# Attention with soft cap and two feed-forward layers: the first pairs' AV product and row sums in column strips, casts on other engines, PSUM banks in one turn

## The chip, the cores and the metric

One core of a Trainium2 chip runs the whole program. The metric is the device time of one execution in microseconds. The times named "before" are those of the unchanged kernel: median 1199.77 us of three runs, from 1199.32 to 1201.66.

## The reference

```python
# q, k, v: (4, 12, 448, 64) float32, cap: a scalar
scores = (q @ k.T) / sqrt(64)
scores = cap * tanh(scores / cap)
attn = exp(scores - max(scores)); attn = attn / (sum(attn) + 1e-9)
x = (attn @ v)                   # heads side by side: (1792, 768)
h = x @ moe_w_in                 # (768, 2048)
x = (h * cos(h)) @ moe_w_out     # (2048, 768)
h = maximum(x @ moe2_w_in, 0)
out = (h * h) @ moe2_w_out       # (1792, 768)
```

## The kernel before

**Precision.** Most products are made of three passes with float32r operands: each operand is split into a high part (a cast) and a low part (operand minus high part), and `mm3` adds high x high, high x low and low x high in PSUM. The exception is the product of the probabilities with v in the first twelve pairs: there both operands are plain float32, and one matmul leaves two records in the trace.

**Pairs.** Two heads make a pair; four batches with six pairs each are 24 pairs, numbered n. Each pair has 448 keys in four groups g: groups 0 to 2 hold 128 keys for each of the two heads, group 3 holds the last 64 keys of both heads, one head in partitions 0 to 63 and the other in 64 to 127. Scores are kept with keys on partitions and the 448 queries along the free axis. The first twelve pairs (n < NA, two batches) are worked off by `a_first` at the start; the other twelve are cut into steps (`a_steps`) that are issued between the matmuls of the feed-forward layers of the first window (`side_step`).

**One call of a_first(n)** issues, in this order: scores of groups 0 and 1; the transposes and casts of pair n+1 (`a_prep`, L298); the loads of pair n+2; exp of groups 0 and 1; the AV product of group 2 of pair n-1; scores of groups 3 and 2; the split of x of pair n-2 (`a_x`, L431); AV of group 3 of pair n-1; the normalisation of pair n-1 (`a_out`, L411); exp of groups 3 and 2; AV of groups 0 and 1 of pair n; the load of v of pair n+1. Between them four slots take pieces of the first three weights' preparation (`W_SLOTS`). Each engine works its instructions off in this order. The scores of groups 0 to 2 are two matmuls beside each other, each in 64 of the 128 rows of the array; those of group 3 use all rows.

**AV before (a_av, L402).** `vf` holds for each head and group 64 columns of v and 64 columns of ones. Each head is a matmul of its own over 128 columns into its own bank: partitions 0 to 63 receive attn @ v, partitions 64 to 127 the sum of exp. `a_out` transposes the sums on VectorE (L417), takes the reciprocal (L422), spreads it with a second transpose (L423) and multiplies (L429), the first and the last once per head. The two banks of a pair, `acc(n)`, alternate between bM and bA; the transposes of pair n+1 use the banks of pair n before its AV begins.

**Casts.** In `a_prep` ScalarE casts k (L327), VectorE casts q and makes both low parts. In `a_x` VectorE makes both parts of x for the first twelve pairs.

**Layers and windows.** A window is two batches. It runs `layer(True)` (cosine gate, eight blocks of 128 features for both batches, sixteen PSUM groups), `layer_out` (back to 768 columns; six column blocks d, two batches b, two steps e), again the same two for the other half of the features, and then the second network's `layer(False)` (ReLU, squared) and `layer_out`, twice. `layer` takes the banks of its ring by the number of the group, `layer_out` by 2d + b; each starts at the ring's first bank. For `layer(True)` the ring has four banks, for `layer(False)` and most calls of `layer_out` three (bM and bS[3]), for the last `layer_out` of a window six. `relu_a` reads a bank on ScalarE (L571). At the end of `layer_out(o_x)`, VectorE makes the high part of x (L631) and GpSimd the low part (L632), which the following `layer(False)` reads.

**Edges.** `a_load`, `a_loadv` and the outputs issue their DMAs on SP's queue. The outputs are transposed (L645), copied by ScalarE and VectorE (L647, L648) and written by two DMAs (L650, L653).

Of the kernel before, what the change touches and what calls it, by code (L numbers as in the profile page):

```python
# [11 lines left out]
F32 = mybir.dt.float32  # L12
# [4 lines left out]
ALU = mybir.AluOpType  # L17
# [11 lines left out]
def tile_softcap_attention_moe_cos_moe_relu2(  # L29
# [59 lines left out]
    bS = [psum.tile([P, 512], F32, name=f"bS{i}") for i in range(4)]  # L89
    bM = [psum.tile([P, 512], F32, name=f"bM{i}") for i in range(2)]  # L90
    bA = [psum.tile([P, 512], F32, name=f"bA{i}") for i in range(2)]

    def hilo(hi, lo, src, eng=None):
        if eng is None:
            nc.scalar.copy(out=hi, in_=src)
        else:
            eng.tensor_copy(out=hi, in_=src)  # L97
        nc.vector.tensor_tensor(out=lo, in0=src, in1=hi.bitcast(F32), op=ALU.subtract)

# [127 lines left out]
    def rows_a(t, b, h, n=1):  # L229
        return t[b, h:h + n, 0:TA, :].rearrange("h (r c) d -> r c h d", c=4)  # L230
# [16 lines left out]
        return t if g < 3 else t[:, 0:1]  # L247


    vf = [at_p.tile([P, 7, P], F32, name=f"vf{i}", tag=("q2", "k2")[i]) for i in range(2)]  # L250

    def v_of(n):
        return vf[n % 2]
# [24 lines left out]
    def a_loadv(n):  # L278
        b, p = divmod(n % (B * NP), NP)
        h = 2 * p  # L280
        if n < NA:
            t = v_of(n)
            for j in range(2):
                nc.sync.dma_start(out=t[0:RA, 3 * j:3 * j + 3, 0:D], in_=rows_a(v, b, h + j)[:, 0:3, 0])
                nc.sync.dma_start(out=t[RA:P, 3 * j:3 * j + 3, 0:D], in_=rows_b(v, b, h + j)[:, :, 0])
                nc.sync.dma_start(out=t[RA * j:RA * j + RA, 6, 0:D], in_=rows_a(v, b, h + j)[:, 3, 0])
            return
        vr = at_p.tile([P, 7, D], F32, name="vr", tag="vr")
        v6 = vr[:, 0:6].rearrange("p (h c) d -> p h (c d)", h=2)
        va = v[b, h:h + 2, 0:TA, :].rearrange("h (r c) d -> r h (c d)", c=4)  # L290
        vb = v[b, h:h + 2, TA:S, :].rearrange("h (r c) d -> r h (c d)", c=3)
        nc.sync.dma_start(out=v6[0:RA], in_=va[:, :, 0:3 * D])
        nc.sync.dma_start(out=v6[RA:P], in_=vb)
        for j in range(2):
            nc.sync.dma_start(out=vr[RA * j:RA * j + RA, 6], in_=rows_a(v, b, h + j)[:, 3, 0])
        vraws[n] = vr

    def a_prep(n):  # L298
        qr, kraw = raws.pop(n), kraw_of(n)
        bq, bk = acc(max(n, 2) - 1) if n < NA else bS[1:3]  # L300
        for t, bank in ((kraw, bk), (qr, bq)):
            for c in range(4):
                nc.tensor.transpose(bank[:, P * c:P * c + P], t[:, c].rearrange("p h d -> p (h d)"), ident)  # L303
        if n >= NA:
            q2 = at_p.tile([P, 2, S], F32R, name="q2", tag="q2")
            k2 = at_p.tile([P, 2, 512], F32R, name="k2", tag="k2")
            hs = [slice(RA * j, RA * j + RA) for j in range(2)]
            for j in range(2):
                nc.scalar.copy(out=k2[hs[j], j], in_=bk[hs[j]])
            for j in range(2):  # L310
                nc.scalar.copy(out=q2[hs[j], j], in_=bq[hs[j], :S])
            for j in range(2):
                nc.gpsimd.tensor_copy(out=k2[hs[1 - j], j], in_=k2[hs[j], j].bitcast(F32))
            for j in range(2):
                nc.vector.tensor_tensor(
                    out=kz[hs[j], j], in0=bk[hs[j]], in1=k2[hs[j], j].bitcast(F32), op=ALU.subtract
                )
            for j in range(2):
                nc.vector.tensor_tensor(
                    out=q2[hs[1 - j], j], in0=bq[hs[j], :S], in1=q2[hs[j], j].bitcast(F32), op=ALU.subtract  # L320
                )
            qkts[n] = (q2, k2)
            return
        t = 2 + 3 * (n % 2)
        qh, ql = gt[t][:, 0], gt[t][:, 1]
        kh, kl = flat[t + 1][:, :512], flat[t + 2][:, :512]
        nc.scalar.copy(out=kh, in_=bk)  # L327
        nc.vector.tensor_copy(out=qh, in_=bq[:, :S])
        nc.vector.tensor_tensor(out=kl, in0=bk, in1=kh.bitcast(F32), op=ALU.subtract)
        nc.vector.tensor_tensor(out=ql, in0=bq[:, :S], in1=qh.bitcast(F32), op=ALU.subtract)  # L330
        qkts[n] = (qh, ql, kh, kl)
# [64 lines left out]
        pts[n, g] = ((vh, ph), (vl, ph), (vh, pl))  # L396

    def a_av(n, g):
        todo = pts.pop((n, g)) if n >= NA else ((v_of(n), t_of(n, g)),)
        for i, (a, x) in enumerate(todo):  # L400
            for j in range(2):
                first, last = g == 0 and i == 0, g == 3 and i == len(todo) - 1  # L402
                if g < 3:
                    nc.tensor.matmul(acc(n)[j][:, :S], a[:, 3 * j + g, :], x[:, j], start=first, stop=last)  # L404
                else:
                    r = slice(RA * j, RA * j + RA)
                    nc.tensor.matmul(acc(n)[j][:, :S], a[r, 6, :], x[r, 0], start=False, stop=last)  # L407

    xts = {}

    def a_out(n):  # L411
        st = at_p.tile([P, S], F32, name="st", tag="st")
        xts[n] = xx = at_p.tile([P, S], F32, name="xx", tag="xx")
        rc = at_p.tile([P, S // 32], F32, name="rc", tag="rc")
        for j in range(2):
            o = slice(RA * j, RA * j + RA)
            nc.vector.transpose(out=st[o], in_=acc(n)[j][RA:P, :S])  # L417
        sums = st.rearrange("p (a b) -> p a b", b=32)[:, :, 0]
        if tops.pop(n, None) is not None:
            nc.vector.tensor_scalar(out=rc, in0=sums, scalar1=1e-9, scalar2=None, op0=ALU.add)  # L420
            sums = rc
        nc.vector.reciprocal(out=rc, in_=sums)  # L422
        nc.vector.transpose(  # L423
            out=st.rearrange("p (a b) -> p a b", b=32),
            in_=rc.rearrange("p (a o) -> p a o", o=1).to_broadcast([P, S // 32, 32]),
        )
        for j in range(2):
            o = slice(RA * j, RA * j + RA)
            nc.vector.tensor_tensor(out=xx[o], in0=acc(n)[j][0:RA, :S], in1=st[o], op=ALU.mult)  # L429

    def a_x(n):  # L431
        b, c = divmod(n, NP)
        if WB <= b < B:
            nc.sync.dma_start(out=xkeep[n - NA], in_=xts.pop(n))
        else:
            hilo(xh[b % WB][c], xl[b % WB][c], xts.pop(n), nc.vector if n < NA else None)

    def x_back(n):
        b = n // NP
# [7 lines left out]
        nc.gpsimd.tensor_tensor(out=xl[b % WB][c], in0=t, in1=xh[b % WB][c].bitcast(F32), op=ALU.subtract)  # L447

    def a_first(n):

        slots = iter(W_SLOTS if n else ((),) * 4)
# [11 lines left out]
            a_exp(n, g)  # L465
        w_slot(next(slots))
        if n > 0:
            a_av(n - 1, 2)
        a_score(n, 3)
        a_score(n, 2)  # L470
        if n > 1:
            a_x(n - 2)
        if n > 0:
            a_av(n - 1, 3)
            a_out(n - 1)
        a_exp(n, 3)
        w_slot(next(slots))
# [1 line left out]
        w_slot(next(slots))  # L479
        for g in range(2):  # L480
            a_av(n, g)
        if 0 < n and n + 1 < B * NP:
            a_loadv(n + 1)

    def a_last(n):
        a_x(n - 1)
        for g in range(2, 4):
            a_av(n, g)
        a_out(n)
        a_x(n)  # L490

# [83 lines left out]
    def split_g(b, i, u):  # L575
        nc.scalar.copy(out=gh[b][i], in_=u)  # L576
        nc.vector.tensor_tensor(out=gl[b][i], in0=u, in1=gh[b][i].bitcast(F32), op=ALU.subtract)  # L577

    def layer(first, weave=None):
        ring = bM + bA if first else bM + bS[3:]  # L580
        w0 = wpos[0]
        order = [(i, b) for i in range(FB) for b in range(WB)]
        if weave is not None:
# [2 lines left out]
        for k, (i, b) in enumerate(order):  # L586
# [3 lines left out]
            elif k == 0:  # L590
                w_next(0)
            wh, wl = wsp[w0 + i]
            ps = ring[k % len(ring)][:, :S]
            for c in range(NCC):
                mm3(ps, wh[:, c], wl[:, c], xh[b][c], xl[b][c], c == 0, c == NCC - 1)
            if weave is not None and k == 2:
# [2 lines left out]
            (cos_a if first else relu_a)(b, i, ps)  # L599
            if k == 0 and weave is not None:  # L600
                weave()

    def layer_out(done, w=None):

        ring = bM + (bS[3:] if w is None else bS)
        w = NWIN if w is None else w
        for d in range(NCC):
            if w + 1 < NWIN:
                for b in range(WB):
                    x_back((w * WB + WB + b) * NP + d)  # L610
            for e in range(FB // OP):
                w_next(WB * OP * 3)
                wh, wl = wsp[wpos[0] - 1]
                for b in range(WB):
                    ps = ring[(WB * d + b) % len(ring)][:, :S]
                    for c in range(OP):
                        f = e * OP + c
                        mm3(ps, wh[:, c], wl[:, c], gh[b][f], gl[b][f], f == 0, f == FB - 1)
# [7 lines left out]
    def o_x(b, d, ps):  # L626
# [2 lines left out]
        nc.scalar.copy(out=u, in_=ps)  # L629
        nc.vector.tensor_tensor(out=t, in0=u, in1=t, op=ALU.add)  # L630
        nc.vector.tensor_copy(out=xh[b][d], in_=t)  # L631
        nc.gpsimd.tensor_tensor(out=xl[b][d], in0=t, in1=xh[b][d].bitcast(F32), op=ALU.subtract)  # L632

    def o_y(w):
        def done(b, d, ps):
# [5 lines left out]
    def y_tr(b, d, y):  # L641
        bk = bA[b % WB]
        for c in range(4):
# [3 lines left out]
        nc.scalar.copy(out=o[0:RA].rearrange("p c f -> p (c f)"), in_=bk[0:RA, :])  # L647
        nc.vector.tensor_copy(out=o[RA:P, 0:3].rearrange("p c f -> p (c f)"), in_=bk[RA:P, 0:3 * P])  # L648
        t0 = (b % B) * S
        nc.sync.dma_start(  # L650
            out=out[t0:t0 + TA, d * P:(d + 1) * P].rearrange("(r c) f -> r c f", c=4), in_=o[0:RA]
        )
        nc.sync.dma_start(  # L653
# [50 lines left out]
    with tc.manual_schedule():  # L704
# [3 lines left out]
            nc.vector.memset(t[0:RA, 3, 1], 0.0)  # L708
        for t in (qraw, wide_view(pg[0])):
            nc.vector.memset(t[RA:P, 3], 0.0)  # L710
        a_load(0)
        busy(11)
        nc.sync.dma_start(out=capt, in_=cap.partition_broadcast(P))
        make_identity(nc, ident)
        a_load(1)
        a_loadv(0)
        for t in vf:
            nc.gpsimd.memset(t[:, :, D:P], 1.0)
        nc.gpsimd.memset(vh[:, :, D:P].bitcast(F32), 1.0)
        nc.gpsimd.memset(vl[:, :, D:P].bitcast(F32), 0.0)  # L720
        nc.vector.scalar_tensor_tensor(
# [50 lines left out]
```

## Time and profile before

| what | value |
|---|---|
| median of three runs | 1199.77 us |
| the profiled execution's own time | 1200.93 us |
| its span | 1199.1 us |
| PE busy | 1180.7 us (98%) |
| PE weight loads busy | 1035.6 us (86%) |
| VectorE busy | 664.0 us (55%) |
| ScalarE busy | 654.1 us (55%) |
| GpSimd busy | 83.4 us (7%) |

The span runs from the first to the last instruction that the profile shows; the rest of an execution's time lies around it. PE is the matmul side of TensorE, PEld its weight loads, DVE is VectorE, ACT ScalarE, POOL GpSimd and SP the engine whose queue issues most DMAs; a "q" behind an engine's name means its sequencer or queue. Matmuls are pipelined: the recorded length of one is more than the distance to the next, so prices of passes are read from the distance between starts. A releaser is the instruction that ended a wait.

### The profile page before, as it was taken

Reading aid. Unit: us, or ns where it says so; the run is one execution under the profiler, and the core shown is the slowest. Engines: PE = TensorE matmul, PEld = TensorE weight load, DVE = VectorE, ACT = ScalarE, POOL = GpSimd, SP = SyncE. Lnnn points to the kernel's source line nnn. Section 1 sums busy time; section 2 is a strip of 40 time slices with the busy share of each in tenths; the row PEclk is TensorE's granted clock in tenths of the full one; section 3 lists DMA queues with packets and bytes.
Section 4 is the critical chain, followed back from the end, with each engine's and each line's share of the span. In section 5 each row is a group of like instructions: output and inputs, shape, how many; then the busy total and the mean of one; then the engine's idle time right before and its main releaser. Section 6 shows DMA issues by size and latency. Waiting matters only on the chain.

```text
span 1199.1 us, 15735 instructions
## 1 busy us (share of the span) xinstructions
PE 1180.7 (98%) x5835; PEld 1035.6 (86%) x5835; DVE 664.0 (55%) x1075; ACT 654.1 (55%) x1092; POOL 83.4 (7%) x86
## 2 busy tenths in 40 slices
PE   9999999999999999999999999999999999999996
PEld 5555899999988888999888999999999998999896
DVE  3886796689999888678777754400442111001121
ACT  6987674377866999677885435512541243124301
POOL 1000000000322110001001210000002100000000
PEclk9999999999999999999999999999999999999998
DMA  5544356754556545556645874234223422342152
GB/s 128 139 101 114 129 201 210 253 212 176 183 161 212 189 145 166 161 167 197 208 148 179 267 238 150 88 105 144 101 72 110 154 88 79 117 139 88 53 150 69
DMA packets 163333, 179.65 MB, mean 150 GB/s; under 512 B 64400, under 2 KB 130464, under 8 KB 163248
## 3 DMA queue, kind: packets, MB, share of 16 engines
q1 hardware_dynamic: 162256, 178.26, 46.9%
q8 instruction: 48, 0.79, 0.3%
q10 hardware_dynamic: 928, 0.23, 0.1%
q14 instruction: 37, 0.30, 0.1%
q0 software_dynamic: 64, 0.07, 0.0%
HBM read 119.93 MB, written 58.59 MB: 149 GB/s over the span
## 4 chain that ended last, share of the span: by engine, by line
PE 94%; DVE 4%; ACT 1%; issue 0%; DVEq 0%
PE bM L524 45%; PE bS L524 23%; PE bA L524 9%; PE bA L404 5%; PE bS L355 3%; PE bS L347 2%; PE bM L404 2%; PE bA L407 1%; PE bS L303 1%; PE bA L645 1%; DVE st L417 1%; DVE xx L429 1%; ACT part L360 0%; PE bM L303 0%; PE bS L700 0%
## 5 line engine op out<-in xcount | busy, mean ns | idle before, releaser
L524 PE MATMUL bM<-g,ws 128*128 128x448 f32 x1344 | 289.7, 368 | 4.8 <-ACT u L571 4.8
L524 PEld LDWEIGHTS bM<-g,ws 128*128 128x128 f32 x1344 | 252.1, 188 | 28.3 <-ACT u L571 6.3
L524 PE MATMUL bM<-xh,ws 128*128 128x448 f32 x912 | 268.3, 366 | 0.2 <-DVE xh L631 0.2
L524 PE MATMUL bS<-g,ws 128*128 128x448 f32 x960 | 210.7, 368 | 0.0
L524 PEld LDWEIGHTS bS<-g,ws 128*128 128x128 f32 x960 | 178.7, 188 | 15.2
L524 PEld LDWEIGHTS bM<-xh,ws 128*128 128x128 f32 x912 | 170.9, 188 | 16.2 <-DVE xh L97 0.7
L577 DVE TENSOR_TENSOR g<-u,g 128x448 fp32r<-128x448 f32 x128 | 80.5, 629 | 165.4 <-ACT g L576 165.4
L524 PE MATMUL bM<-xl,ws 128*128 128x448 f32 x456 | 167.4, 367 | 1.4 <-POOL xl L632 1.4
L524 PE MATMUL bA<-xh,ws 128*128 128x448 f32 x372 | 108.7, 366 | 0.0
L561 DVE SCALAR_TENSOR_TENSOR u<-kk,u 128x448 f32<-128x448 f32 x64 | 39.9, 624 | 123.5 <-ACT kk L560 123.0
L169 ACT CAST ws<-wf 128x512 fp32r<-128x512 f32 (+1 forms) x80 | 56.3, 704 | 72.6 <-DVE wf L162 28.3
L170 DVE TENSOR_TENSOR ws<-wf,ws 128x512 fp32r<-128x512 f32 (+1 forms) x80 | 64.1, 801 | 57.3 <-ACT ws L169 55.9
L524 PEld LDWEIGHTS bM<-xl,ws 128*128 128x128 f32 x456 | 85.4, 187 | 9.5 <-POOL xl L632 1.7
L576 ACT CAST g<-u 128x448 fp32r<-128x448 f32 x128 | 71.6, 560 | 8.7 <-DVE u L566 6.9
L524 PE MATMUL bS<-xh,ws 128*128 128x448 f32 x252 | 76.1, 367 | 0.0
L524 PEld LDWEIGHTS bA<-xh,ws 128*128 128x128 f32 x372 | 69.8, 188 | 6.0
L360 ACT ACTIVATE pg<-bS,small 128x448 f32<-128x448 f32 x102 | 59.4, 635 | 20.5 <-PE bS L355 15.7
L524 PE MATMUL bA<-xl,ws 128*128 128x448 f32 x186 | 68.1, 366 | 0.0
L162 DVE CUSTOM_DVE_ANT_0 wf<-wr,wf 128x1024 uint16<-128x1024 uint16 (+1 forms) x80 | 64.7, 808 | 2.0
L159 DVE SCALAR_TENSOR_TENSOR wf<-wr,wf 128x512 uint32<-128x512 uint32 (+1 forms) x80 | 63.7, 796 | 1.7
L154 ACT ACTIVATE wf<-wr 128x512 f32<-128x512 f32 (+1 forms) x80 | 61.4, 768 | 0.1
L624 ACT COPY part<-bM 128x448 f32<-128x448 f32 x32 | 17.1, 534 | 81.4 <-PE bM L524 81.3
(129 smaller groups left out, 1522.4 us busy)
## 6 DMA issues: line engine op xcount, KB each, us to landing
wr<-in_moe_w_in_dram SPq DMA_DIRECT2D x32, 768.0 KB, 4.8
wkeep<-ws SPq DMA_DIRECT2D x32, 768.0 KB, 3.6
wr<-in_moe_w_out_dram SPq DMA_DIRECT2D x48, 512.0 KB, 3.8
wkeep<-ws SPq DMA_DIRECT2D x48, 512.0 KB, 3.5
ws<-wkeep SPq DMA_DIRECT2D x32, 768.0 KB, 4.3
ws<-wkeep SPq DMA_DIRECT2D x48, 512.0 KB, 3.8
out_dram<-o SPq DMA_DIRECT2D x24, 128.0 KB, 2.6
qraw<-in_q_dram SPq DMA_DIRECT2D x22, 128.0 KB, 2.7
```

Source lines behind the costliest of these rows:

```text
L154: lambda: nc.scalar.activation(out=f, in_=r.bitcast(F32)[:, :n, 1], func=AF.Copy, scale=2.0 ** -112),
L159: lambda: nc.vector.scalar_tensor_tensor(out=u, in0=hi, scalar=0x80000000, in1=u, op0=ALU.bitwise_and, op1=ALU.bitwise_or),
L162: lambda: nc.vector.tensor_tensor(out=u, in0=u, in1=lo, op=ALU.add),
L169: nc.scalar.copy(out=t[:, 0], in_=f)
L170: nc.vector.tensor_tensor(out=t[:, 1], in0=f, in1=t[:, 0].bitcast(F32), op=ALU.subtract)
L355: nc.tensor.matmul(bk[j][:, :S], k[:, j, cols], q2[:, j], start=(i == 0 and (g < 3 or j == 0)), stop=(i == 1 and (g < 3 or j == 1)),)
L360: nc.scalar.activation(out=t_of(n, g)[:, j], in_=bk[j][:, :S], func=AF.Tanh, scale=tsc)
L404: nc.tensor.matmul(acc(n)[j][:, :S], a[:, 3 * j + g, :], x[:, j], start=first, stop=last)
L524: nc.tensor.matmul(o, l, r, start=start, stop=stop)
L561: nc.vector.scalar_tensor_tensor(out=u, in0=kk, scalar=MAGIC, in1=u, op0=ALU.subtract, op1=ALU.subtract)
L576: nc.scalar.copy(out=gh[b][i], in_=u)
L577: nc.vector.tensor_tensor(out=gl[b][i], in0=u, in1=gh[b][i].bitcast(F32), op=ALU.subtract)
```

## The change

- **AV of the first pairs.** `vf` holds both heads' v side by side (4 groups of 128 columns); in group 3 it is block-diagonal, with zeros that VectorE sets once. For groups 0 to 2 each head is a matmul into 64 columns, both into one bank, in partitions 0 to 63 and 64 to 127. Group 3 is one matmul over all rows and columns. The sums of exp are matmuls of their own (`a_sums`) against 32 columns of ones, two groups and two heads at a time in four strips of 32 columns, into the pair's second bank.
- **Order.** Group 3 of the pair before comes ahead of the scores of group 3, and the sums and group 2 behind the scores of group 2.
- **a_out** makes one transpose over all partitions, adds the two halves of each head's sum with four small additions, and multiplies once.
- **Engines.** For n of 2 to 11 VectorE casts k. For n under 10 GpSimd makes x's low part, for 10 and 11 VectorE. In `o_x` VectorE makes the low part of the last column block.
- **Banks.** `layer` and `layer_out` draw banks from one counter that goes on from one to the next, and is set to 0 around `layer(True)` and before the last `layer_out`, whose ring begins with two banks of bS.
- **DMAs.** v of a pair is loaded with five DMAs instead of six; the first of the last two output DMAs is issued by ScalarE.

```diff
-    vf = [at_p.tile([P, 7, P], F32, name=f"vf{i}", tag=("q2", "k2")[i]) for i in range(2)]
+    vf = [at_p.tile([P, 4, P], F32, name=f"vf{i}", tag=("q2", "k2")[i]) for i in range(2)]
+    ones = [t.bitcast(F32) for t in (vh[:, 0, D:D + 32], kz[:, 0, 0:32], kz[:, 1, 0:32])]
...
-            for j in range(2):
-                nc.sync.dma_start(out=t[0:RA, 3 * j:3 * j + 3, 0:D], in_=rows_a(v, b, h + j)[:, 0:3, 0])
-                nc.sync.dma_start(out=t[RA:P, 3 * j:3 * j + 3, 0:D], in_=rows_b(v, b, h + j)[:, :, 0])
-                nc.sync.dma_start(out=t[RA * j:RA * j + RA, 6, 0:D], in_=rows_a(v, b, h + j)[:, 3, 0])
+            th = t[:, 0:3].rearrange("p c (h d) -> p c h d", h=2)
+            nc.sync.dma_start(out=th[RA:P], in_=rows_b(v, b, h, 2))
+            for j in range(2):
+                o = slice(RA * j, RA * j + RA)
+                nc.sync.dma_start(out=th[0:RA, :, j], in_=rows_a(v, b, h + j)[:, 0:3, 0])
+                nc.sync.dma_start(out=t[o, 3, o], in_=rows_a(v, b, h + j)[:, 3, 0])
...
-        nc.scalar.copy(out=kh, in_=bk)
+        if n < 2:
+            nc.scalar.copy(out=kh, in_=bk)
+        else:
+            nc.vector.tensor_copy(out=kh, in_=bk)
...
+        if n < NA:
+            av, t = acc(n)[0], t_of(n, g)
+            if g == 3:
+                nc.tensor.matmul(av[:, :S], v_of(n)[:, 3], t[:, 0], start=False, stop=False)
+                return
+            for j in range(2):
+                o = slice(RA * j, RA * j + RA)
+                nc.tensor.matmul(av[o, :S], v_of(n)[:, g, o], t[:, j], start=(g == 0), stop=(g == 2))
+            return
...
+    def a_sums(n, k):
+        for j in range(2):
+            for i, c in enumerate((2 * k, 2 * k + 1)):
+                o = slice(RA * j + 32 * i, RA * j + 32 * i + 32)
+                x = t_of(n, c)[:, j if c < 3 else 0]
+                nc.tensor.matmul(acc(n)[1][o, :S], ones[0 if c < 3 else 1 + j], x, start=(k == 0), stop=(k == 1))
...
+        if n < NA:
+            nc.vector.transpose(out=st, in_=acc(n)[1][:, :S])
+            for i in range(4):
+                o, e = (slice(32 * c, 32 * c + 32) for c in (i, i ^ 1))
+                nc.vector.tensor_tensor(out=rc[o], in0=sums[o], in1=sums[e], op=ALU.add)
+            sums = rc
...
+        if n < NA:
+            nc.vector.tensor_tensor(out=xx, in0=acc(n)[0][:, :S], in1=st, op=ALU.mult)
+            return
...
-            hilo(xh[b % WB][c], xl[b % WB][c], xts.pop(n), nc.vector if n < NA else None)
+            x = xts.pop(n)
+            eng = nc.scalar.copy if n >= NA else nc.vector.tensor_copy
+            eng(out=xh[b % WB][c], in_=x)
+            eng = nc.gpsimd if n < NA - 2 else nc.vector
+            eng.tensor_tensor(out=xl[b % WB][c], in0=x, in1=xh[b % WB][c].bitcast(F32), op=ALU.subtract)
...
         if n > 0:
-            a_av(n - 1, 2)
+            a_av(n - 1, 3)
         a_score(n, 3)
         a_score(n, 2)
         if n > 1:
             a_x(n - 2)
         if n > 0:
-            a_av(n - 1, 3)
+            a_sums(n - 1, 1)
+            a_av(n - 1, 2)
             a_out(n - 1)
...
         for g in range(2):
             a_av(n, g)
+        a_sums(n, 0)
...
+    turns = [0]
+    def bank(ring):
+        turns[0] += 1
+        return ring[(turns[0] - 1) % len(ring)][:, :S]
...
-            ps = ring[k % len(ring)][:, :S]
+            ps = bank(ring)
...
-        ring = bM + (bS[3:] if w is None else bS)
-        w = NWIN if w is None else w
+        ring = bM + bS[3:] if w is None else bS[:2] + bM + bS[2:]
+        if w is None:
+            w = NWIN
+        else:
+            turns[0] = 0
...
-                    ps = ring[(WB * d + b) % len(ring)][:, :S]
+                    if e == 0:
+                        sums.append(bank(ring))
+                    ps = sums[b]
...
-        nc.gpsimd.tensor_tensor(out=xl[b][d], in0=t, in1=xh[b][d].bitcast(F32), op=ALU.subtract)
+        eng = nc.vector if d == NCC - 1 else nc.gpsimd
+        eng.tensor_tensor(out=xl[b][d], in0=t, in1=xh[b][d].bitcast(F32), op=ALU.subtract)
...
-        nc.sync.dma_start(
+        eng = nc.scalar if b % B == B - 1 and d == NCC - 1 else nc.sync
+        eng.dma_start(
             out=out[t0:t0 + TA, d * P:(d + 1) * P].rearrange("(r c) f -> r c f", c=4), in_=o[0:RA]
...
+        for t in vf:
+            for j in range(2):
+                nc.vector.memset(t[RA * (1 - j):RA * (1 - j) + RA, 3, RA * j:RA * j + RA], 0.0)
...
-        for t in vf:
-            nc.gpsimd.memset(t[:, :, D:P], 1.0)
+        for j in range(2):
+            nc.gpsimd.memset(ones[1 + j][RA * j:RA * j + RA], 1.0)
```

## Rows read from the trace of the kernel before

**Rows 1.** The page, busy time of the engines

```profile
PE 1180.7 (98%) x5835; PEld 1035.6 (86%) x5835; DVE 664.0 (55%) x1075; ACT 654.1 (55%) x1092; POOL 83.4 (7%) x86
```

**Rows 2.** Waits of PE over the span: total us, times, longest us

```profile
PE bM L524 <- ACT u L571: 4.8, 4, 2.9
...
PE bM L524 <- POOL xl L632: 1.4, 1, 1.4
```

**Rows 3.** Chain of waits, first pairs: start us, us, what

```profile
32.83 3.20 PE bM L404 x8
...
65.06 0.63 DVE xx L429
...
65.73 1.09 PE bM L303 x8
...
89.31 3.20 PE bM L404 x8
...
98.61 3.21 PE bA L404 x8
```

**Rows 4.** Timeline of PE, single passes of the first pairs' AV

```profile
98.54 0.64 PE L404 MATMUL bA<-part,vf 128*128 128x448 f32 x1
99.02 0.54 PE L404 MATMUL bA<-part,vf 128*128 128x448 f32 x1
99.40 0.54 PE L404 MATMUL bA<-part,vf 128*128 128x448 f32 x1
...
107.01 0.54 PE L407 MATMUL bA<-pg,vf 64*128 64x448 f32 x2
107.38 0.54 PE L407 MATMUL bA<-pg,vf 64*128 64x448 f32 x2
107.85 0.64 PE L404 MATMUL bM<-part,vf 128*128 128x448 f32 x1
```

**Rows 5.** Groups by line, 0 to 120 us: busy us, mean ns

```profile
L429 DVE TENSOR_TENSOR xx<-bM,st 64x448 f32<-64x448 f32 x12 | 7.4, 617 | 0.3
...
L329 DVE TENSOR_TENSOR g<-bM,g 128x512 fp32r<-128x512 f32 x5 | 3.5, 692 | 1.6 <-ACT g L327 1.6
...
L422 DVE RECIPROCAL rc<-st 128x14 f32<-128x14 f32 x11 | 2.7, 243 | 0.4
```

**Rows 6.** Windows of one pair: us, then busy PE, PEld, DVE, ACT, POOL

```profile
45.30:54.60 9.30, 9.16 (x46) 5.39 (x45) 8.01 (x14) 8.42 (x14) 0.00 (x0) 1.00 0.37 81
89.10:98.41 9.31, 9.31 (x47) 5.42 (x45) 6.20 (x11) 7.41 (x13) 0.00 (x0) 1.00 0.33 75
```

**Rows 7.** Timeline around the first window's layer(False): VectorE, GpSimd, PE

```profile
387.68 0.40 DVE L631 CAST xh<-part 128x448 fp32r<-128x448 f32 x1
...
388.86 1.56 DVE L630 TENSOR_TENSOR part<-u,part 128x448 f32<-128x448 f32 x1
...
388.22 1.71 POOL L632 TENSOR_TENSOR xl<-part,xh 128x448 fp32r<-128x448 f32 x1 [5.08 <-DVE xh L631]
...
389.99 0.47 PE L524 MATMUL bM<-xl,ws 128*128 128x448 f32 x1 [1.39 <-POOL xl L632]
```

**Rows 8.** Timeline of PE, then windows with the granted clock as last but two

```profile
477.64 4.18 PE L524 MATMUL bM<-g,ws 128*128 128x448 f32 x12 [2.92 <-ACT u L571]
...
944.71 2.62 PE L524 MATMUL bS<-g,ws 128*128 128x448 f32 x12
...
478.50:481.80 3.30, 3.30 (x11) 2.89 (x10) 2.06 (x4) 1.72 (x3) 0.00 (x0) 0.50 0.77 274
...
1007.50:1010.00 2.50, 2.50 (x14) 2.30 (x13) 0.63 (x1) 0.50 (x1) 0.00 (x0) 1.00 0.61 210
```

**Rows 9.** Timeline of the end: the last copy and the last DMA issue

```profile
1191.09 0.56 DVE L648 COPY o<-bA 64x384 f32<-64x384 f32 x1 [0.44 <-ACT o L647]
...
1192.03 0.90 SPq L653 DMA_DIRECT2D out_dram<-o  x1
```

**Rows 10.** Timeline of PE's weight loads, one pass of the first pairs' AV

```profile
99.02 0.19 PEld L404 LDWEIGHTS bA<-part,vf 128*128 128x128 f32 x1 [0.19 <-issue]
```

More of the change, by code (lines that the diff above doesn't have):

```diff
@@ L91, in tile_softcap_attention_moe_cos_moe_relu2 @@
     bA = [psum.tile([P, 512], F32, name=f"bA{i}") for i in range(2)]
[L93 to L98, printed above, removed]
     wseq = []
@@ L398, in a_av @@
     def a_av(n, g):
-        todo = pts.pop((n, g)) if n >= NA else ((v_of(n), t_of(n, g)),)
-        for i, (a, x) in enumerate(todo):
-            for j in range(2):
-                first, last = g == 0 and i == 0, g == 3 and i == len(todo) - 1
+        if n < NA:
[3 more added lines that the diff above has]
+                return
+            for j in range(2):
+                o = slice(RA * j, RA * j + RA)
+                nc.tensor.matmul(av[o, :S], v_of(n)[:, g, o], t[:, j], start=(g == 0), stop=(g == 2))
+            return
+        for i, (a, x) in enumerate(pts.pop((n, g))):
+            for j in range(2):
+                first, last = g == 0 and i == 0, g == 3 and i == 2
                 if g < 3:
@@ L414, in a_out @@
         rc = at_p.tile([P, S // 32], F32, name="rc", tag="rc")
-        for j in range(2):
-            o = slice(RA * j, RA * j + RA)
-            nc.vector.transpose(out=st[o], in_=acc(n)[j][RA:P, :S])
         sums = st.rearrange("p (a b) -> p a b", b=32)[:, :, 0]
+        if n < NA:
[6 more added lines that the diff above has]
+            for j in range(2):
+                o = slice(RA * j, RA * j + RA)
+                nc.vector.transpose(out=st[o], in_=acc(n)[j][RA:P, :S])
         if tops.pop(n, None) is not None:
@@ L486, in a_last @@
         a_x(n - 1)
-        for g in range(2, 4):
-            a_av(n, g)
+        a_av(n, 3)
+        a_sums(n, 1)
+        a_av(n, 2)
         a_out(n)
@@ L577, in split_g @@
         nc.vector.tensor_tensor(out=gl[b][i], in0=u, in1=gh[b][i].bitcast(F32), op=ALU.subtract)
+    turns = [0]
+    def bank(ring):
+        turns[0] += 1
+        return ring[(turns[0] - 1) % len(ring)][:, :S]
     def layer(first, weave=None):
         ring = bM + bA if first else bM + bS[3:]
+        if first:
+            turns[0] = 0
         w0 = wpos[0]
@@ L601, in layer @@
                 weave()
+        if first:
+            turns[0] = 0
     def layer_out(done, w=None):
-        ring = bM + (bS[3:] if w is None else bS)
-        w = NWIN if w is None else w
+        ring = bM + bS[3:] if w is None else bS[:2] + bM + bS[2:]
+        if w is None:
+            w = NWIN
+        else:
+            turns[0] = 0
         for d in range(NCC):
@@ L610, in layer_out @@
                     x_back((w * WB + WB + b) * NP + d)
+            sums = []
             for e in range(FB // OP):
```

## The prediction

> **What bounds the kernel now.** I read the page's busy line first: the matmul side of TensorE is busy for 98% of the span, VectorE and ScalarE for 55% each [rows 1]. So only two things can shorten the run: fewer or denser passes through the array, and the few places where the array stands still. Second, the waits of PE: they add up to under 10 us, and most of it is one group, 4.8 us in four waits for the ReLU read of a PSUM bank, then 1.4 us for GpSimd's xl [rows 2]. Third, the chain of waits in the stretch of the first twelve pairs, whose probabilities meet v in plain float32. The eight AV passes that close a pair start at 89.31 and again at 98.61, a period of 9.30 us made of PE alone; from 32.83 to 89.31 lie six periods of 9.41 us, and there the chain leaves PE for VectorE and comes back just as the transposes start (65.06 DVE, 65.73 PE) [rows 3]. So in the first pairs PE is the limit, with VectorE level with it while weights are being prepared. Fourth, single passes in the timeline. A float32 matmul leaves two records. Two passes over the whole array start 0.38 us apart (99.02, 99.40). Two heads in the two row halves start together ("x2") and the next two 0.37 us later (107.01, 107.38): abreast, at the price of one. A change of shape costs at both ends: from half-row to whole-array the starts lie 0.47 us apart (107.38, 107.85), 0.10 over the normal 0.37, and behind the first whole-array pass 0.48 (98.54, 99.02), again 0.10 over. That is about 0.2 us a change [rows 4].
>
> **Part 1, the first pairs' AV.** I count passes one after the other. Before: three key groups x two heads x two records = 12, and the fourth group's two heads in row halves = 2; 14 x 0.375 = 5.25 us a pair. After: groups 0 to 2 with each head in 64 columns, two abreast: 3 x 2 = 6; the fourth group as one whole-array matmul: 2; the sums of exp, formerly the spare columns of v, now eight small matmuls per pair in 32-column strips, four abreast: 2 x 2 = 4. Together 12 x 0.375 = 4.5 us, 0.75 less. Shape changes: before four a pair (half-row, whole, half-row, whole); after six (half-row scores, whole, half-row, 32 columns, 64 columns, 32 columns, half-row). Two more x 0.2 = 0.4. Net 0.35 us x 12 pairs = 4.2 us.
>
> No column strip is in the trace of before, so this has bounds. If the four changes that touch a column shape are free, a pair gains 0.75 + 0.4 = 1.15 us (13.8 in all); if each costs 0.4, it loses 0.45 (5.4 in all). I take 0.2, the nearest row. If strips don't run abreast at all, the passes become 12 + 16 + 2 = 30, 11.25 us, and the stage loses 6.4 x 12 = 77 us. I take abreast, because the row halves are, in the same data type and with the same two records [rows 4].
>
> **Part 2, VectorE beside it.** The pairs with weight work lose 0.11 us x 6 = 0.6 us to VectorE [rows 3]. What does it do afterwards? One multiplication replaces two of 0.62, and one transpose two, counted alike; xl leaves it (0.6); it gets the k cast (0.69, as the subtraction of the same 512 columns) and four additions of 14 columns, each under the 0.24 of the reciprocal, above nothing [rows 5]. Sum: -0.6 - 0.6 - 0.6 + 0.7 + (0 to 1.0), between -1.1 and -0.1 a pair; I take -0.5. Its busy time was 6.20 us in a plain pair and 8.01 in one with weights [rows 6], so 5.7 and 7.5 of a new period of 8.95. The cast of k no longer waits behind four tanh, and the row sums no longer wait for the last AV pass. Hence the 0.6 us goes too. What speaks against it: beside a GpSimd subtraction of 1.71 us a VectorE addition took 1.56 us, where its neighbours of that length take 0.62 [rows 5, 7]; xl on GpSimd can so cost VectorE 0.95 us in a pair, which makes 8.5, still under 8.95. Queued behind it are the row sums and then the transposes of the pair after next, which need the bank freed; PE is the one who would wait. ScalarE loses a cast and has 7.41 of 9.31 us busy [rows 6]: nothing. SP has one DMA issue fewer per pair: nothing. The four new memsets on VectorE at the start fall where it waits for the cap: nothing; if that cover were gone, under 1 us.
>
> **Part 3, the banks in one turn.** layer(False) takes sixteen turns on a ring of three, so its last group lands in the first bank, and layer_out began with the first bank again: it waited for the ReLU to read it. With one counter the next bank is the one used three groups earlier; and the last layer_out begins in two banks that only attention uses, long done by then. All four waits go: 4.8 us [rows 2]. The long one has a second price. After it twelve matmuls took 4.18 us, where the same twelve take 2.62 elsewhere; the granted clock from 478.5 to 481.8 was 0.50, the lower of its two levels (1.2 GHz) [rows 8]. Without the stall before it the clock has no reason to fall, as it didn't after one of the other three waits, of 0.6 us each (1.00 from 1007.5 on): 1.6 us more. What is late next? In that stretch ScalarE is full, and the next AV passes of the interleaved attention need its splits; I leave 0.1 us for it. Part 3: 6.3 us. Bounds: 3 us if that backlog comes back as another wait, 6.5 us if nothing does.
>
> **Part 4, the edges.** xl of the last column block moves to VectorE. The cast ended at 388.08, GpSimd's subtraction at 389.93, PE went on at 389.99 [rows 7]. A subtraction of 0.62 right behind the cast ends near 388.75: 1.2 us saved, in one window; what it pushes back is one weight operation that nobody awaits there. The last output DMA: its copy ended at 1191.65 and SP issued it at 1192.03, behind the other one [rows 9]; with that one on ScalarE's queue 0.3 us goes.
>
> **Sum.** 4.2 + 0.6 + 6.3 + 1.2 + 0.3 = 12.6 us. From the profiled execution's 1200.93 us (span 1199.1, 1.8 around it) that is 1188.3; the median shown is 1.16 below that execution, so the forecast is 1187.2.
>
> **Rivals.**
> (a) Slower: the strips don't run fully abreast, since all of them take in all 128 rows, and each has its own stream to read. Four in two turns of two: 4 passes more, 1.5 us x 12 = 18 us, 1205; none abreast: 77 + 4.2 = 81 us more than forecast, about 1268. It decides from 12.6 / 12 = 1.05 us a pair, that is from 0.48 us for each of the ten column passes instead of 0.375. For it: nothing in the trace shows a column strip. Against it: the loads of weights of the next pass run while the array streams through the same 128 rows (99.02, 0.19 us, within the pass of 99.02) [rows 10], so sharing rows is no bar to a load. The Trainium skill, "TensorE: Matmul & The Clock Gate", The mechanism, says that weight loads overlap with running matmuls only when the row groups differ. Taken literally it gives the 1268; the trace disagrees for the whole-array shape.
> (b) Strips abreast, but each set slower than one pass, up to that break-even: 1187 to 1200, the middle 1194. Against it: the row halves pay nothing [rows 4]. The same page, Measured speedup vs the span model, has 2.38 for three column tiles and 3.07 for four row tiles; my estimate from it is passes 1.26 to 1.3 times as long, which would be 1199 to 1201. By the rows the row halves reach twofold, so I don't use it.
> (c) VectorE becomes the limit of the first pairs, held by GpSimd's port use: from a period of 9.3 the stage gains nothing, 1187.2 + 4.8 = 1192. For it: the chain passed through VectorE in six pairs. Against it: 8.5 of 8.95 at worst.
> (d) Column changes are free: 9.6 us more, 1177.6. For it: smaller weight loads to wait for. Against it: every change in the trace costs.
> (e) The bank turn doesn't do what it says, and ScalarE's backlog stalls PE a few passes later: 1190.5. Against it: two of the four boundaries lie in the second window, which has no attention beside its layers.
>
> **How the numbers follow.** Forecast 0.58; (a) 0.12, (b) 0.07, (c) 0.10, (d) 0.07, (e) 0.06. The likeliest case has its own range, 1184 to 1191, from its unknown shape changes and VectorE terms. For 8 in 10 I go from 1179 to 1199: outside are (a), most of (d) and the end of (b), some 0.18. 0.2% is 2.4 us, about what a measurement of this kernel tells from no change: faster means under 1197.4. All but (a) and the upper end of (b) are: 0.84; within it 0.04; slower 0.12.
>
> **What would show it.** The AV passes of two heads should start within some ns of each other, and four sums likewise; the period of the first pairs should be near 8.95 us, and the first layer should start some 5 us earlier. PE should have no wait left for the ReLU, and the granted clock should stay at 1.00 through the first window. If column passes follow each other at 0.375 us each head, (a) is true. If the period is 9.3 and the chain runs through VectorE, (c) is. If the stage gains much more than 5 us, the price of a shape change was wrong.

## The result and the profile after

The changed kernel takes 1188.05 us (median of 4 runs, 1186.79 to 1189.01), the kernel before 1200.62 us on the same chip: ratio 0.9895, 95% interval 0.9878 to 0.9912. The profiled execution took 1186.79 us, with a span of 1184.9.

The page's busy line after, with PE now at 99%:

```profile
PE 1171.9 (99%) x6003; PEld 1021.0 (86%) x6003; DVE 657.5 (55%) x1107; ACT 648.9 (55%) x1082; POOL 88.3 (7%) x92
```

The waits of PE after (total us, times, longest):

```profile
PE bS L356 <- ACT pg L361: 1.8, 1, 1.8
...
PE bM L559 <- DVE xh L683: 0.2, 1, 0.2
...
PE bM L559 <- DVE xl L686: 0.2, 1, 0.2
```

Against [rows 2]: the four waits for the ReLU are gone, GpSimd's 1.4 us too, and a wait of 1.8 us on ScalarE that the kernel before did not have has come.

The chain of waits after, first pairs: the eight 64-column passes that close a pair, against [rows 3].

```profile
57.62 1.50 PE bA L408 x8
...
66.41 1.50 PE bM L408 x8
...
75.19 1.50 PE bA L408 x8
```

The period is 8.79 us instead of 9.30 to 9.41, also in the pairs with weight work, where no link of the chain is VectorE's any more. (Two early pairs took 8.94 and 8.87 us: there the two heads' 64-column passes start 0.14 and 0.09 us apart instead of together. Why is not known.) The timeline of PE after, against [rows 4]: four sums, AV of one group, then the way back to 32 columns and to half rows.

```profile
82.11 0.56 PE L425 MATMUL bA<-pg,vh 128*32 128x448 f32 x1
82.12 0.56 PE L425 MATMUL bA<-pg,kz 128*32 128x448 f32 x1
82.13 0.56 PE L425 MATMUL bA<-pg,vh 128*32 128x448 f32 x1
82.13 0.56 PE L425 MATMUL bA<-pg,kz 128*32 128x448 f32 x1
82.51 0.54 PE L425 MATMUL bA<-pg,vh 128*32 128x448 f32 x1
...
83.00 0.60 PE L408 MATMUL bA<-pg,vf 128*64 128x448 f32 x2
83.43 0.55 PE L408 MATMUL bA<-pg,vf 128*64 128x448 f32 x2
...
84.18 0.55 PE L408 MATMUL bM<-part,vf 128*64 128x448 f32 x2
...
84.93 0.55 PE L408 MATMUL bM<-part,vf 128*64 128x448 f32 x2
85.41 0.58 PE L425 MATMUL bM<-part,vh 128*32 128x448 f32 x4
85.81 0.56 PE L425 MATMUL bM<-part,vh 128*32 128x448 f32 x4
86.30 0.47 PE L348 MATMUL bS<-g,g 64*128 64x448 f32 x2
```

Four strips start within 0.02 us and make one slot: 0.40 us later the next four start, of which 0.03 belongs to the change before them (E4 shows 0.37 between sets further from a change). Two 64-column passes make one slot of 0.375 (84.18 to 84.93 is two). What a change costs is what lies over 0.375: 0.11 into 64 columns (82.51, 83.00) and 0.05 behind it, 0.10 into 32 (84.93, 85.41) and 0.03 behind it, 0.11 from 32 to half rows (85.81, 86.30) and 0.10 behind it.

To compare kernels I cut each trace at the same matmuls, the first of each layer and each layer_out in the timeline of PE; a stretch is the difference of two starts. "Start" is where the second head's scores of the first pair begin after VectorE's casts (chain of waits: 9.75 before, 8.68 after). Times in us:

| stretch | before | after | E1 AV only | E2 banks only | E3 sums 64 | E4 sums once | E5 xl GpSimd | E6 tail SP | E7 casts back | E8 E4+E5 |
|---|---|---|---|---|---|---|---|---|---|---|
| start | 9.75 | 8.68 | 8.57 | 8.60 | 9.45 | 8.62 | 8.60 | 9.37 | 9.13 | 9.41 |
| first pairs | 109.34 | 103.63 | 103.85 | 109.59 | 117.68 | 101.89 | 103.62 | 103.88 | 103.93 | 101.89 |
| layer, out, layer | 178.70 | 179.47 | 179.46 | 178.70 | 179.14 | 180.24 | 179.47 | 179.47 | 179.49 | 180.24 |
| layer_out(o_x) | 85.02 | 85.04 | 85.05 | 85.02 | 85.03 | 85.05 | 85.04 | 85.04 | 85.09 | 85.05 |
| layer(False) and the wait behind it | 94.83 | 91.99 | 94.74 | 91.64 | 91.99 | 92.01 | 91.67 | 91.99 | 92.03 | 91.67 |
| its layer_out | 91.04 | 89.29 | 90.95 | 89.29 | 89.29 | 89.29 | 89.29 | 89.29 | 89.39 | 89.29 |
| rest of window 1 | 142.08 | 141.13 | 142.03 | 141.13 | 141.11 | 141.13 | 141.13 | 141.11 | 141.16 | 141.13 |
| window 2 to its last layer_out | 414.74 | 413.04 | 414.74 | 413.04 | 413.04 | 413.04 | 413.04 | 413.04 | 413.05 | 413.04 |
| last layer_out to the end | 73.65 | 72.64 | 74.62 | 73.47 | 72.61 | 72.60 | 72.70 | 74.31 | 72.64 | 72.65 |

After less before: -1.07, -5.71, +0.77, +0.02, -2.84, -1.75, -0.95, -1.70, -1.01, together -14.2, as the spans differ. The first term is no work of the change: the granted clock rose to its higher level at 7.43 us before and at 5.14 after, and in all the profiles here somewhere between 4.3 and 7.6. The start follows it: 8.57 to 8.68 us in the five kernels where the clock rose by 5.2, 9.37 to 9.81 in the six where it rose after 6.6, the kernel before among them. The other 13.2 us stand against 12.6 by the medians.

### The profile page after: what moved, and what is told of

It reads as the page before. It is cut to its first block, busy times and chain, and to the rows that moved or that the text cites. A ratio compares the mean times of both kernels' runs of the same rounds, so it can differ in the third digit from the quotient of the medians.

```text
span 1184.9 us, 16063 instructions
## 1 busy us (share of the span) xinstructions
PE 1171.9 (99%) x6003; PEld 1021.0 (86%) x6003; DVE 657.5 (55%) x1107; ACT 648.9 (55%) x1082; POOL 88.3 (7%) x92
## 4 chain that ended last, share of the span: by engine, by line
PE 97%; ACT 1%; DVE 1%; issue 0%
PE bM L559 46%; PE bS L559 23%; PE bA L559 10%; PE bA L414 4%; PE bS L356 3%; PE bS L348 3%; PE bM L408 1%; PE bA L408 1%; PE bA L425 1%; PE bM L425 1%; PE bS L301 1%; PE bA L699 1%; PE bA L417 1%; PE bA L301 1%; PE bM L301 0%; PE bA L404 0%
## 5 line engine op out<-in xcount | busy, mean ns | idle before, releaser
L155 DVE CUSTOM_DVE_ANT_0 wf<-wr,wf 128x1024 uint16<-128x1024 uint16 (+1 forms) x80 | 64.6, 808 | 1.9
```

What stands on the lines that cost most here:

```text
L155: lambda: nc.vector.tensor_tensor(out=u, in0=u, in1=lo, op=ALU.add),
```

## The experiments

**E1 and E2: each half alone.** E1 is the changed kernel with the banks, `o_x` and the last DMA as before; E2 is the kernel before with the counter for the banks and nothing else (part of its edit):

```diff
+        turns[0] += 1
+        return ring[(turns[0] - 1) % len(ring)][:, :S]
...
-            ps = ring[k % len(ring)][:, :S]
+            ps = bank(ring)
...
-        ring = bM + (bS[3:] if w is None else bS)
+        ring = bM + bS[3:] if w is None else bS[:2] + bM + bS[2:]
```

> The changed kernel with the banks, the edge in o_x and the last DMA put back as before; only the first pairs' part stays. Theory (forecast's part 1 and 2): the stage of the first twelve pairs gains 4.8 us, by the profile after 5.7 (period 8.79 instead of 9.3): time 5 to 6 us under before, ratio 0.9950 to 0.9958; the four waits for the ReLU and the drop of the granted clock near the first window's middle come back. Rival (the gain of the whole is the banks', the first pairs gain nothing because VectorE limits them): ratio 0.999 or more, period 9.3.

> The kernel before with the one counter for the banks and nothing else. Theory (forecast's part 3): the four waits (4.8 us) and the stretch at the lower clock level (1.6 us) go, 6.3 us under before, ratio 0.9948; no wait of PE on the ReLU, granted clock 1.00 from the first microseconds to the end. Rival (ScalarE's backlog returns as another wait): 3 us, ratio 0.9975, with a wait of PE on ScalarE of 2 to 3 us in the same layer_out.

E1: 1196.44 us against 1200.53, ratio 0.9965 (0.9951 to 0.9978). That is 4.1 us by the medians, less than the 5 to 6 expected. By the table the first pairs gained 5.5 us, so the rival without a gain there is out; 0.8 was lost again in the layers behind them, and its end fell 1.0 us longer. Its waits of PE, and the granted clock (last but two) behind the long one:

```profile
PE bM L559 <- ACT u L606: 4.8, 4, 2.9
```

```profile
472.20:475.20 3.00, 3.00 (x9) 2.66 (x9) 2.06 (x4) 2.05 (x4) 0.00 (x0) 0.50 0.66 227
```

E2: 1192.31 us, ratio 0.9934 (0.9920 to 0.9948), 8.2 us less where 6.3 were expected. No wait for the ReLU is left in it, and in the same place the clock stays:

```profile
473.60:476.60 3.00, 3.00 (x17) 2.76 (x15) 2.33 (x4) 2.95 (x6) 0.00 (x0) 1.00 0.47 147
```

By the table the banks give 3.19 + 1.75 + 0.95 + 1.70 = 7.6 us; the rival with the returning backlog is out. The stall of 2.9 us, then, is what goes before the lower clock: the level fell behind it in both kernels that have it, and in the middle of none of the ten profiled without it. The waits of 0.6 us (before and E1) and of 1.8 us (after) were not followed by a fall.

**E3: the sums in two strips of 64.** The ones are 64 columns wide, each group's two heads beside each other, no additions in `a_out`:

```diff
-        for j in range(2):
-            for i, c in enumerate((2 * k, 2 * k + 1)):
-                o = slice(RA * j + 32 * i, RA * j + 32 * i + 32)
+        for c in (2 * k, 2 * k + 1):
+            for j in range(2):
+                o = slice(RA * j, RA * j + RA)
```

> The changed kernel with the sums in two strips of 64 columns instead of four of 32: eight pass slots a pair for the sums instead of four, four changes of shape instead of six, no additions in a_out. Theory (a slot costs 0.375 us however many strips run in it, a change about 0.12 us): 4 x 0.375 - 2 x 0.12 = 1.26 us more a pair, 15 us in all, 1203, period 10.05. Rival (four strips abreast cost more than two, so half of it comes back): 5 to 8 us more, 1195.

1201.64 us, ratio to before 1.0011 (1.0002 to 1.0020): all of the first pairs' gain is gone and more. Its chain of waits:

```profile
54.33 1.50 PE bM L408 x8
...
64.37 1.50 PE bA L408 x8
```

A period of 10.04 us, as the slots and changes add up (four slots more at 0.375, two changes fewer at 0.12). So a slot costs the same for two strips as for four, and four abreast is what makes the new sums cheap. E4, where four sets of four strips follow each other, shows it without a sum, by the starts of its third and fourth set:

```profile
90.28 0.54 PE L425 MATMUL bM<-part,kz 128*32 128x448 f32 x1
...
90.65 0.54 PE L425 MATMUL bM<-part,kz 128*32 128x448 f32 x1
```

**E4: a pair's sums at one place**, one change of shape fewer:

```diff
+            a_sums(n - 1, 0)
             a_sums(n - 1, 1)
...
             a_av(n, g)
-        a_sums(n, 0)
```

> The changed kernel with all four groups' sums of a pair at one place, ahead of AV of group 2 of the pair before: five changes of shape a pair instead of six, the same passes, but the normalisation starts 0.75 us later. Theory (a change into or out of 32 columns costs 0.1 to 0.15 us and PE is the limit): period 8.65, 1.5 us less, ratio 0.9988 of the changed kernel. Rival (the later normalisation holds up the transposes that need its bank): period 8.79 or more, no gain.

1186.51 us, ratio to before 0.9886 (0.9871 to 0.9902). The chain:

```profile
48.80 1.50 PE bM L408 x8
...
57.45 1.50 PE bA L408 x8
```

8.65 us instead of 8.79: a change costs 0.13 us, and the later normalisation holds up nothing in these pairs. With the 0.77 us of sums that moved into the first layer the stretches give 1.0 us instead of the 1.5 expected; the medians alone can't tell that from the changed kernel. The missing half is in the opening pair: there the chain stays on ScalarE up to 15.47 us (13.02 in the changed kernel), and the passes that close the second pair start 0.55 us later (22.80 against 22.25). The sums that were moved away had filled part of a wait for ScalarE, as it seems; that was not tried.

**E5: the low part of the last column block back on GpSimd.**

```diff
-        eng = nc.vector if d == NCC - 1 else nc.gpsimd
-        eng.tensor_tensor(out=xl[b][d], in0=t, in1=xh[b][d].bitcast(F32), op=ALU.subtract)
+        nc.gpsimd.tensor_tensor(out=xl[b][d], in0=t, in1=xh[b][d].bitcast(F32), op=ALU.subtract)
```

> The changed kernel with the low part of x of the last column block back on GpSimd. The forecast's part 4 has VectorE's subtraction worth 1.2 us: undone, the layer's xl wait of 1.4 us comes back and the time goes up by 1.2 us, 1189.2. Rival (read after the result: the same weight preparation holds up ScalarE's tanh either way, so PE waits for one or the other): the xl wait of 1.4 us comes back, the wait of 1.8 us on ScalarE goes, the first layer(False) with the layer_out's end takes 91.6 us instead of 92.0, time 0.3 us less, ratio to the changed kernel 0.9997.

1187.82 us, ratio to before 0.9896 (0.9879 to 0.9912), not to be told from the changed kernel by the median; by the stretch 91.67 against 91.99, and E2 with GpSimd has 91.64. The waits of PE in E5:

```profile
PE bM L559 <- POOL xl L685: 1.4, 1, 1.4
```

The 1.8 us on ScalarE are absent. PE waits for one or the other, and VectorE's subtraction costs 0.3 us instead of saving 1.2: the seven kernels with it (after, E3, E4, E6, E7, E9, E10) have 91.99 to 92.07 us in that stretch, the three with the new banks and GpSimd (E2, E5, E8) 91.64 to 91.67.

**E6: both last DMAs on SP's queue**, as before (`nc.sync` in place of `eng`).

> The changed kernel with the last output DMAs both on SP's queue, as before. Forecast's part 4: 0.3 us more, 1188.3. Rival (read in the profiles: from the start of the last layer_out to the end the kernels with SP alone took 73.4 to 74.6 us, those with ScalarE's queue 72.6): 0.9 to 2 us more, 1189 to 1190.

1189.17 us, ratio to before 0.9902 (0.9886 to 0.9919). The end of it and, below, of the changed kernel: the last copy and the last issues.

```profile
1178.73 0.56 DVE o L702
...
1179.68 1.62 SPq L708 DMA_DIRECT2D out_dram<-o  x1
```

```profile
1177.80 0.56 DVE L702 COPY o<-bA 64x384 f32<-64x384 f32 x1 [0.44 <-ACT o L701]
...
1177.80 0.59 ACTq L706 DMA_DIRECT2D out_dram<-o  x1
...
1178.39 0.53 SPq L709 DMA_DIRECT2D out_dram<-o  x1
```

The issue came 0.39 us after the copy, as in [rows 9]; with both queues 0.03 us after it. So the issue brings the 0.36 us that it was forecast to. But from the last layer_out to the end the kernels with SP alone took 73.5 to 74.6 us, those with both queues 72.6 to 72.7: 0.8 to 2 us, and less spread. What goes beyond 0.36 lies behind the last issue, and its cause wasn't tried. The medians of E6 and the changed kernel, 1.1 us apart, can't tell them from each other; the stretch rests on one profile of each kernel.

**E7: the casts of the first pairs back on their old engines** (k on ScalarE for all n, x's low part on VectorE for all):

```diff
-        if n < 2:
-            nc.scalar.copy(out=kh, in_=bk)
-        else:
-            nc.vector.tensor_copy(out=kh, in_=bk)
+        nc.scalar.copy(out=kh, in_=bk)
...
-            eng = nc.gpsimd if n < NA - 2 else nc.vector
-            eng.tensor_tensor(out=xl[b % WB][c], in0=x, in1=xh[b % WB][c].bitcast(F32), op=ALU.subtract)
+            nc.vector.tensor_tensor(out=xl[b % WB][c], in0=x, in1=xh[b % WB][c].bitcast(F32), op=ALU.subtract)
```

> The changed kernel with k cast by ScalarE in every pair and x's low part by VectorE, so the first pairs keep only the new matmuls. Theory (PE alone limits the first pairs, other engines have room): period 8.78 us, same time within 0.3 us. Rival (in the six pairs with weight work VectorE is the limit again without the two moves): period 9.0 to 9.2 there, 1.5 to 2.5 us more, 1190, and the chain of those pairs passes through VectorE.

1188.39 us, ratio to before 0.9903 (0.9886 to 0.9919). Its chain, in the pairs with weight work:

```profile
49.56 1.50 PE bM L405 x8
...
58.36 1.50 PE bA L405 x8
...
67.15 1.50 PE bM L405 x8
```

Periods of 8.80 and 8.79 us, PE alone. The first of them, and the six pairs with weight work together, by engine (columns as in [rows 6]):

```profile
49.56:58.36 8.80, 8.80 (x61) 4.31 (x59) 6.68 (x15) 8.80 (x15) 0.00 (x0) 1.00 0.69 168
...
31.50:84.72 53.22, 53.22 (x356) 26.21 (x356) 43.15 (x93) 49.32 (x79) 0.00 (x0) 1.00 0.52 125
```

One early pair took 9.30 us (31.48 to 40.78), with PE alone in the chain: its two heads' passes start 0.45 us apart, as they did by less in the two early pairs of the changed kernel. The two moves are worth nothing here, and the hold of GpSimd's subtraction on VectorE that they bring (below) costs nothing. But the other engines have less room than was expected: ScalarE shows no idle time in the first period, so it stands level with PE there.

**E8: E4 and E5 together.**

> The changed kernel with all four sums of a pair at one place and the low part of the last column block on GpSimd. Theory: the 1 us that the profile of the first of these two showed (period 8.66, less 0.75 us moved into the first layer) and 0.3 us of the second, 1.3 us less than the changed kernel, 1186.7, ratio to it 0.9989. Rival: within 0.3 us of the changed kernel.

1186.07 us (1185.41 to 1186.23), ratio to before 0.9876 (0.9860 to 0.9893), the fastest kernel here; its interval overlaps that of the changed kernel, and the stretches give it 1.3 us less, as expected.

**E9 and E10: the order at the close of the last first pair**, after an open question that the table raised. Behind the first pairs the three long stretches of the first network's layers run slower in the changed kernel: one and the same 36 matmuls take 7.32 us in the chain of before (203.3 ns each) and 7.36 after (204.4).

```profile
162.53 7.32 PE bA L524 x36
```

```profile
163.14 7.36 PE bM L559 x36
```

```diff
-        a_av(n, 3)
         a_sums(n, 1)
+        a_av(n, 3)
         a_av(n, 2)
```

(E10 has the whole-array pass last.)

> The changed kernel; only the close of the last first pair, inside the first layer, has another order: sums, whole-array pass, 64-column passes. Open question: the first three layers run at 204.4 ns a matmul in the kernels with 32-column strips and at 203.3 in those without. Theory A (the last changes of shape before a long stretch of equal matmuls set its pace): 203.3 or another pace than 204.4, the three stretches behind the first layer 58.56 instead of 58.88 us. Theory B (it comes from the strips in the stage before): 204.4 as in the changed kernel.

> As the one before, with the order sums, 64-column passes, whole-array pass, so that no column strip stands right ahead of the layer's matmuls. Theory A: the pace differs from 204.4. Theory B: 204.4, and the first layer's stretch 0.05 to 0.1 us shorter at most, because one change of shape fewer stands in it.

A single run of each, 1188.58 and 1188.88 us. Both have 58.88 us in each of the two stretches behind the first layer, as the changed kernel. Theory A is out. The first layer's own stretch is 61.72 us in E10, as in the changed kernel (61.71), not 0.05 to 0.1 shorter. B isn't shown by that: all nine kernels with 32-column strips have 58.88 there, the three without 58.56, but at the end of the run every kernel has 58.88, those too. The cause stays open.

## Why the prediction was right

The forecast was 1187.2 us, the result 1188.05. The 12.6 us forecast are the 12.6 between the medians; the 0.85 us between forecast and result are the kernel before's own, 1200.62 us in the comparison and 1199.77 in the forecast. The sum held, its terms less.

**Part 1, AV.** Right in kind; together with part 2's 0.6 us the term was 0.9 us too small. The twelve slots at 0.375 came as counted. Two things were mis-sized. A change of shape into and between column strips costs 0.12 to 0.16 us, and 0.2 only back to half rows, instead of 0.2 throughout; so the period is 8.79, not 8.95. Over twelve pairs that would be some 6.8 us in place of 4.8, but the stage gains 5.7, because the gain doesn't come twelve times. The pair that closes the stage has no transposes beside it, and its chain now passes through ScalarE's tanh:

```profile
101.54 1.50 PE bM L408 x8
...
104.77 1.68 ACT part L361 x3
...
109.98 1.50 PE bA L408 x8
```

That is 8.44 us; before, with PE alone in the chain, it was 8.48:

```profile
107.92 3.20 PE bM L404 x8
...
116.40 3.20 PE bA L404 x8
```

The step behind the opening pair went from 9.34 us (14.18 to 23.52) to 9.18 (13.07 to 22.25) only. The forecast had ScalarE at nothing in all twelve pairs. Rival (a) is refuted by the starts of the strips (82.11 to 82.13), (b) by the 0.375 between slots; (d) by E4, where one change less still saves 0.13. The rule in the Trainium skill, "TensorE: Matmul & The Clock Gate", The mechanism, that weight loads overlap running matmuls only where row groups differ, would have made (a) true; strips that all use the 128 rows ran four abreast, so it doesn't hold for them here.

**Part 2, VectorE.** The limit went from the six pairs, as said. Of the two reasons given, the cast of k is not needed: E7 has both casts back and the same period. That the row sums no longer wait for the last AV pass is not tried by itself; E4, whose sums come 0.75 us later, loses nothing in those pairs. What is left is the shorter `a_out`, one transpose and one multiplication instead of two each: VectorE's busy time in the six pairs with weight work is 43.15 us in E7, and before it was 47.80:

```profile
32.83:89.31 56.48, 56.06 (x272) 32.53 (x271) 47.80 (x80) 49.75 (x79) 0.00 (x0) 1.00 0.48 119
```

So this cause is argued from what is left; no run has it alone. VectorE's load, from windows of one pair after (columns as in [rows 6]), is near the 7.5 and 5.7 forecast:

```profile
48.84:57.62 8.78, 8.78 (x62) 4.32 (x59) 7.72 (x17) 8.66 (x15) 0.16 (x1) 1.00 0.66 166
83.97:92.76 8.79, 8.79 (x62) 4.31 (x59) 5.51 (x14) 7.14 (x13) 1.14 (x1) 1.00 0.36 81
```

GpSimd's hold on VectorE was there, at 0.5 us instead of the 0.95 feared: the first small addition took 0.66 us where the next takes 0.17, and it ended (58.64) just behind GpSimd's subtraction (57.46 + 1.14 = 58.60).

```profile
57.98 0.66 DVE L438 TENSOR_TENSOR rc<-st 32x14 f32<-32x14 f32 x1
58.65 0.17 DVE L438 TENSOR_TENSOR rc<-st 32x14 f32<-32x14 f32 x1
...
57.46 1.14 POOL L469 TENSOR_TENSOR xl<-xx,xh 128x448 fp32r<-128x448 f32 x1 [9.10 <-DVE xh L466]
```

The Trainium skill, "SBUF — State Buffer", SBUF: two separate sides, has it as a lock for a whole instruction between a GpSimd operation that reads SBUF and a VectorE operation with two SBUF inputs; this trace agrees. VectorE had slack enough, so rival (c) did not come.

**Part 3, banks.** Right, and 1.3 us too small. The drop of the clock was read rightly (1.75 us against 1.6). The waits were priced by PE's recorded idle time, 0.63 us for a short one, but the stretches shrank by 0.79 to 0.83 each, and by 3.2 around the long one; the passes beside a stall lose time that isn't recorded as idle (behind GpSimd's wait in [rows 7] a pass is recorded with 0.47 us, where its like takes 0.36). Rival (e) did not come.

**Part 4, the edges.** Here a step failed. The forecast had VectorE's subtraction push back "one weight operation that nobody awaits there". The timeline after shows who awaits it:

```profile
382.03 0.62 DVE L686 TENSOR_TENSOR xl<-part,xh 128x448 fp32r<-128x448 f32 x1
382.57 0.95 DVE L155 CUSTOM_DVE_ANT_0 wf<-wr,wf 128x1536 uint16<-128x1536 uint16 x1
...
383.56 0.83 ACT L162 CAST ws<-wf 128x768 fp32r<-128x768 f32 x1 [4.31 <-DVE wf L155]
384.30 0.90 ACT L147 ACTIVATE wf<-wr 128x768 f32<-128x768 f32 x1
385.10 1.15 ACT L361 ACTIVATE pg<-bS,small 128x448 f32<-128x448 f32 x2
...
385.77 0.47 PE L356 MATMUL bS<-q,k 128*128 128x448 f32 x1 [1.79 <-ACT pg L361]
```

In E5, where the weight operation (L155) comes first, ScalarE's cast of the weights waits less:

```profile
382.84 0.83 ACT L162 CAST ws<-wf 128x768 fp32r<-128x768 f32 x1 [3.65 <-DVE wf L155]
```

ScalarE stood idle for 4.3 us at that cast, with the tanh behind it, and the next scores needed the tanh's bank. 0.66 us of it come from the subtraction; the other 3.65 were there before, hidden behind PE's wait for xl. So 1.2 us forecast became 0.3 us lost (E5). The other edge, the last DMA, was forecast at 0.3 us, by the issue alone. The issue brought 0.36, the end as a whole 0.8 to 2 (E6).

**What no step had.** The layers behind the first pairs lost 0.8 us, of which 0.6 is the slower pace of two stretches. Against the forecast the terms of the profiles stand at +0.9, +1.3 and +0.7 gained, 1.5 and 0.8 lost, together 0.6 over the 12.6: a close total out of five misses, and so in part luck.

## What to carry to other kernels

Count passes in slots: matmuls that fill disjoint column strips cost one slot together, so small products (row sums above all) should be packed four abreast, and shapes put side by side, since each change costs 0.1 to 0.2 us. At every seam between loops look which bank the last turn used and which the next begins with; a stall of 2.9 us there was followed by a stretch at half the clock, which cost 1.75 us more. Before you speed up what the chain waits for, follow the queue of every engine that the faster step pushes back, to the next wait that the old one was hiding.

## What the runs showed that I had not expected

One and the same stream of matmuls ran at two paces at the granted clock of 1.00: 203.3 and 204.4 ns a matmul (58.56 and 58.88 us for 288), steady within a stretch and the same in every kernel of the same kind. The time at which the granted clock rises at the start moved between 4.3 and 7.6 us from profile to profile, which moves the whole run by up to 1.2 us: more than several edits here are worth, and a reason to compare stretches instead of spans.
